# Key-value products of two token tiles in one run: eight runs instead of sixteen

## The chip, the cores and the metric

The kernel runs on one core of one Trainium2 chip. A core has a matrix engine (TensorE, PE in the profile; its weight loads are shown apart, as PEld), a vector engine (VectorE, DVE), a scalar engine (ScalarE, ACT), a general engine (GpSimd, POOL), and a queue engine that issues most transfers (SyncE, SP). Each works through its own list of instructions in order and waits on semaphores for the others. The metric is the device time of one execution, in microseconds; lower is better.

## The reference

The inputs are 2048 tokens of 640 numbers in float32. They are normalised over the 640; then two branches use the result, and the output combines them.

```python
xn = _layernorm(x, axis=-1)
s = _A_ref(xn, A_wqkv, A_w_phi, A_wo)          # attention branch
g = _silu(_B_ref(xn, B_w1, B_b1, B_w2, B_b2))  # 640 -> 1536 -> 640 with gelu
return x + s * g
```

The attention branch has 32 heads of 20 numbers and no softmax over tokens. Queries and keys go through a small weight per head and then through two softmaxes over the head's 20 numbers, one of the positive and one of the negative values, which gives 40 features per head. Keys and values meet in one sum over all tokens:

```python
phi_k = jnp.concatenate([_softmax(pk, axis=-1), _softmax(-pk, axis=-1)], axis=-1)
kv = jnp.einsum("bhsf,bhsd->bhfd", phi_k, v)
z  = jnp.einsum("bhsf->bhf", phi_k)
num = jnp.einsum("bhqf,bhfd->bhqd", phi_q, kv)
den = jnp.einsum("bhqf,bhf->bhq", phi_q, z)[..., None] + 1e-6
```

`kv` and `z` are 40 x 21 numbers per head, summed over 2048 tokens. This sum is what the change touches.

## The kernel before

The tokens are cut into 16 tiles of 128. The kernel has a first stage, in which keys, values and query features are made tile by tile, a feed-forward stage of 12 units (L870 on), and a last stage that forms the outputs. The first stage is the subject here.

For token tile t the first stage does the following. `project(t, wk_s)` (L323 to L336) makes the key projection with 30 matmuls of 320 columns, into a PSUM tile pA of two banks (`bankA`); there are three such tiles (`open_psum(early_psum, A=3, B=2)`, L79). `feat1` (L341) reads pA on VectorE (maximum L345, minimum L346, difference L349, L352) and makes the second half of the features on GpSimd (L353); L349 is the last to read pA. `value(t)` (L374) makes the value projection in another pA, which ScalarE copies to a row tile v (L380) with a column of ones per head, so that the same products give `z`. `feat2` takes the exponential on ScalarE (L358). `key_fin` (L389) sums per head on VectorE (L366), inverts (L391) and scales on GpSimd (L371); the result, phi, stays where e was. `query(t)` (L383) is a projection with `wq_s`, the same features, and a store to DRAM from ScalarE's queue (L385).

`kv_acc(t, phi, v)` (L395) then adds the tile to the sum. It issues 32 small matmuls: 128 tokens deep, 32 columns of weights from v, 40 moving columns from phi, each into one of four groups of 32 partitions of one PSUM bank (`kv`). They are in full float32, and each is shown in the profile as two matmuls and two weight loads, so that one call is 64 of each. The first call of all clears the sum (`start=t == 0`). Each of the 16 calls is one unbroken run at L403.

The order of the work is written out by hand, for all engines, in the order of the program text (`manual_schedule`, L462 and L468). Tiles 0 and 1 come first (L499 to L520), tiles 2 to 5 in one loop (L521), tiles 6 to 15 in another (L543). Before the change, the runs stand as follows: tile t - 2 after the key projection of tile t, for t = 2 to 5; tile 4 after the key projection of t = 6; and tile t - 1 at the end of each t from 6 on, behind a query projection (two query projections in t = 6, one in front and one behind in t = 7 to 9). Tile 15 is left for `kv_rest` (L597), after the loop, which also copies the sum out on ScalarE (L603). Around them stand the folds of the query weights (`fold_w`, L178: matmuls at L173, copies at L183 and L184), the statistics of later token tiles (`pair_stats`, L286: L197 to L202, L200 on GpSimd, a store to DRAM at L293 and a load of it back at L295, both on SyncE), the loads of token tiles (`x_in`, L455, issued at L141 on SyncE), and, for the second half of the tokens, the transposed x (xr, L231; subtracted at L301, multiplied at L306, split at L252 and L254) and its sums (tt, L267 and L284).

What sets the slots: the pool `slabs` (L50) has 23 slots, for the split weights, the features e and phi, xr, tt and the b12 pieces; the pool `rows` (L51) has 11, for token tiles, raw weights, v and the broadcast statistics. A slot is given out again when its last reader is done; the new writer waits for that reader.

The first feed-forward unit begins right behind the last query projection, with `part` (L640, matmuls at L650) on weights that `w1_forms` splits at the end of the loop (L415 to L427).

Of the kernel before, what the change touches and what calls it, by code (L numbers as in the profile page):

```python
# [16 lines left out]
NT = S // P  # L17
# [29 lines left out]
def hedgehog_gated_mlp_kernel(ctx: ExitStack, tc: tile.TileContext, x, xt_in, wqk, bd, wv, wo, w1, b1, w2, b2, out_t):  # L47
# [103 lines left out]
    def load_raw(src, blk=None):  # L151
        raw = row([P, D], F32, "raw")
        dst = raw[:] if blk is None else raw[:].rearrange("p (a b) -> p a b", b=blk)
        nc.sync.dma_start(dst, src)
        return raw
# [22 lines left out]
    def fold_w(tl, cs, name, dst):  # L178
        for c in cs:
            ps, mm = fold(tl, c)  # L180
            sl = slab(F32R, f"{name}{c}")
            s3 = sl[:].rearrange("p s (a b) -> p s a b", a=2)
            nc.scalar.activation(s3[:, 0], ps[:, :, :HALF], AF.Copy)  # L183
            lo = nc.vector.tensor_tensor(s3[:, 1], ps[:, :, :HALF], s3[:, 0].bitcast(F32), op=OP.subtract)  # L184
            dst.append(sl)
        return mm, lo
# [35 lines left out]
    def norm(t):  # L222
        norm_a(t)
        norm_b(t)
# [36 lines left out]
    def spill(q):  # L261
        nc.sync.dma_start(xp_dram[:, :8, :, at(q)], xp[:, :, :, at(q)].bitcast(F32))
        nc.sync.dma_start(xp_dram[:, 8:, :, at(q)], beside(q).bitcast(F32))
# [22 lines left out]
    def pair_stats(t):  # L286
        if t % 2 == 0:
            pst[0] = small.tile([P, 2, 2], F32, tag="pst", name="pst")
        sm = small.tile([P, 16], F32, tag="st", name="st")
        stats(t, sm, pst[0][:, t % 2, 0:1], pst[0][:, t % 2, 1:2])  # L290
        if t % 2:
            q = t // 2
            nc.sync.dma_start(st_dram[q].rearrange("i p s -> p i s"), pst[0][:])  # L293
            bc = row([P, W2, 2], F32, "bc")
            nc.sync.dma_start(bc[:].rearrange("p t s -> p (t s)"),  # L295
                              st_dram[q].rearrange("i p s -> (i p s)").partition_broadcast(P))
            pld[q] = bc
# [14 lines left out]
    def transpose_x(t):  # L312
        q, o = divmod(t, 2)
        xn = xns.pop(t)
        ps = bankA()
        flat = ps[:].rearrange("p a b -> p (a b)")
        for k in range(KC):
            nc.tensor.transpose(flat[:, k * P:(k + 1) * P], xn[:, k * P:(k + 1) * P], ident[:])  # L318
        plain(q, o, flat[:, :D].rearrange("p (k t) -> p k t", t=P))
# [3 lines left out]
    def project(t, ws, mid=None, at_k=3):  # L323
        q, o = divmod(t, 2)
        ps = bankA()
        n = 0
        for k in range(KC):
            if k == at_k and mid is not None:
                mid()
            for a, b in PASSES:  # L330
                for hf in range(2):
                    nc.tensor.matmul(ps[:, hf, :HALF], stat_x(q, o, k, a),  # L332
                                     ws[k][:, b, hf * HALF:(hf + 1) * HALF],
                                     start=n == 0, stop=n == 3 * KC - 1)
                n += 1
        return ps  # L336
# [4 lines left out]
    def feat1(ps):  # L341
        p4 = heads(ps)
        mx = small.tile([P, 2, 16], F32, tag="mx", name="mx")
        mn = small.tile([P, 2, 16], F32, tag="mn", name="mn")
        nc.vector.tensor_reduce(mx[:], p4, axis=AX.X, op=OP.max)  # L345
        nc.vector.tensor_reduce(mn[:], p4, axis=AX.X, op=OP.min)  # L346
        e = slab(F32, "e")[:]
        e5 = e.rearrange("p a (h s d) -> p a h s d", s=2, d=DH)
        nc.vector.tensor_tensor(e5[:, :, :, 0, :], p4, mx[:, :, :, None].to_broadcast([P, 2, 16, DH]),  # L349
                                op=OP.subtract)  # L350
        nr = small.tile([P, 2, 16], F32, tag="nr", name="nr")
        last_feat[0] = nc.vector.tensor_tensor(nr[:], mn[:], mx[:], op=OP.subtract)  # L352
        nc.gpsimd.tensor_tensor(e5[:, :, :, 1, :], nr[:, :, :, None].to_broadcast([P, 2, 16, DH]),  # L353
                                e5[:, :, :, 0, :], op=OP.subtract)
        return e.rearrange("p a b -> p (a b)")

    def feat2(ef):
        nc.scalar.activation(ef, ef, AF.Exp)  # L358
        return ef
# [14 lines left out]
    def value(t, mid=None):  # L374
        ps = project(t, wv_s, mid)
        v = row([P, VW], F32, "v")
        v3 = v[:, :32 * (DH + 1)].rearrange("p (h d) -> p h d", d=DH + 1)
        nc.gpsimd.memset(v3[:, :, DH:DH + 1], 1.0)
        nc.gpsimd.memset(v[:, 32 * (DH + 1):], 0.0)
        nc.scalar.activation(v3[:, :, :DH].rearrange("p (a h) d -> p a h d", a=2), heads(ps), AF.Copy)  # L380
        return v
# [13 lines left out]
    def kv_acc(t, phi, v):  # L395
        ps = kvp[0]
        for g in range(3):
            for r in range(3):
                for e in range(4):
                    h = 3 * (4 * g + e) + r  # L400
                    if 4 * g + e < NFT and h < H:
                        s = 3 * g + r
                        nc.tensor.matmul(ps[32 * e:32 * e + 32, 40 * s:40 * s + 40], v[:, 21 * h:21 * h + 32],  # L403
                                         phi[:, 40 * h:40 * h + 40], start=t == 0 and s == 0, stop=t == NT - 1,
                                         skip_group_check=True)

    vs, es, phis, xns, wk_s, wq_s = {}, {}, {}, {}, [], []

    def load_w1(g):
        return [load_raw(w1[f]) for f in range(g * GF, (g + 1) * GF)]  # L410

# [43 lines left out]
    def x_in(t):  # L455
        xts[t] = load_x(t)
# [63 lines left out]
    phis[1] = key_fin(es.pop(1))  # L520
    for t in range(2, 6):  # L521
        pk = project(t, wk_s)
        kv_acc(t - 2, phis.pop(t - 2), vs.pop(t - 2))
        es[t] = feat1(pk)
        if t == 5:
            fold_w(wqT, range(2, 3), "wq", wq_s)
        if t < 4:
            norm(t + 3)
        if t == 3:
            norm(7)  # L530
        if t > 3:
            pair_stats(t + 4)
        if t in (3, 4):
            spill(t - 3)
        if t == 5:
            x_in(10)
        vs[t] = value(t, (lambda: transpose_x(t + 2)) if t < 6 else None)
        feat2(es[t])
        if t >= 3:
            fold_w(wqT, range(t - 3 + (t > 4), t - 2 + (t > 4)), "wq", wq_s)  # L540
        phis[t] = key_fin(es.pop(t))
    queries = iter(range(NT))
    for t in range(6, NT):  # L543
        u = t + 4
        pk = project(t, wk_s)
        if t == 6:
            kv_acc(4, phis.pop(4), vs.pop(4))
        if u < NT:
            if u + 1 < NT:
                x_in(u + 1)  # L550
            pair_stats(u)
            if u % 2:
                load_xr(u // 2)
        if t in (6, 8):
            spill(t // 2 - 1)
        if t % 2 == 0 and 6 < t < NT - 2:
            pair_sub((t + 2) // 2)
        es[t] = feat1(pk)
        if t == 6:
            pair_sub(4)  # L560
            fold_w(wqT, range(4, KC), "wq", wq_s)
        if t % 2 == 0 and t < NT - 2:
            pair_mul((t + 2) // 2)
        if t == 12:
            w1r = load_w1(0)
        if t % 2 and t < NT - 2:
            t_sums((t + 1) // 2)
        vs[t] = value(t)
        feat2(es[t])
        phis[t] = key_fin(es.pop(t))  # L570
        if t % 2 == 0 and 6 < t < NT - 2:
            pair_plain((t + 2) // 2)
        if t % 2 and t < NT - 2:
            t_split((t + 1) // 2)
        if t == 6:
            query(next(queries))
            query(next(queries))
            pair_plain(4)
        if t == NT - 1:
            w1f = w1_forms(w1r)  # L580
            next(w1f)
            next(w1f)
        if t >= 7:
            query(next(queries))
        kv_acc(t - 1, phis.pop(t - 1), vs.pop(t - 1))
        if t == NT - 1:
            next(w1f)
        if 7 <= t < 10:
            query(next(queries))
    t = NT - 1  # L590
# [4 lines left out]
    w1g = next(w1f)  # L595

    def kv_rest():  # L597
        kv_acc(NT - 1, phis.pop(NT - 1), vs.pop(NT - 1))
        kvr = const.tile([P, 360], F32, name="kvr")
        nc.gpsimd.memset(kvr[64:96, 320:360], 0.0)  # L600
        nc.gpsimd.memset(kvr[96:, 240:360], 0.0)
        for p, a, b in ((P, 0, 240), (96, 240, 320), (64, 320, 360)):
            nc.scalar.activation(kvr[:p, a:b], kvp[0][:p, a:b], AF.Copy)  # L603
        return kvr
# [265 lines left out]
    for unit in range(units):  # L870
# [10 lines left out]
        if more and not back:  # L881
            w1r = load_w1((unit + 1) % NG)
# [206 lines left out]
```

## Time and profile before

| | |
|---|---|
| median of the runs | 684.15 us |
| lowest and highest of three runs | 682.97 and 684.3 us |
| profiled execution, first to last instruction (the span) | 681.1 us |
| the median less that span | 3.05 us |
| TensorE busy, share of the span | 676.4 us, 99% |
| VectorE, GpSimd, ScalarE busy | 454.8, 382.2, 253.0 us |
| granted TensorE clock | 1.000 |

The page gives the profiled execution by its span; what a run takes beside it is the third difference above. A row of the timeline is start, duration, engine, line, operation, the tile written and the tiles read, the shape and the count; in square brackets stands the idle time before it and what ended it. Matmuls overlap, so a TensorE that is shown as busy may still be slowed; the distance between the starts of two matmuls tells more than their durations. A row of the chain is start, duration, engine, tile, line and count.

### The profile page before, as it was taken

How to read it: one execution, taken by the hardware profiler on the slowest of the kernel's cores; microseconds unless marked ns; L12 is line 12 of the kernel's file. 1: busy time of each engine (PE TensorE's matmuls, PEld its weight loads, DVE VectorE, ACT ScalarE, POOL GpSimd, SP SyncE). 2: the span in 40 equal slices, each digit the busy share in tenths (PEclk: the TensorE clock that was granted, in tenths of full speed). 3: DMA queues.
4: the chain of work that ended last, by engine and by line, in shares of the span. 5: the costliest groups of instructions: out<-in, count | busy, mean ns of one | idle time of the engine just before them, and what ended most of it. 6: DMA issues, size and time to landing. Idle time of an engine off the chain costs nothing.

```text
span 681.1 us, 11991 instructions
## 1 busy us (share of the span) xinstructions
PE 676.4 (99%) x4727; PEld 592.0 (87%) x4727; DVE 454.8 (67%) x729; ACT 253.0 (37%) x400; POOL 382.2 (56%) x351
## 2 busy tenths in 40 slices
PE   9999999999999999999999999999999999999998
PEld 9999999999999998888888888888888887777876
DVE  5786665887876466586978784576876655774232
ACT  3523214333223337144254247533133254425440
POOL 3653254757767375857978952726446640783221
PEclk9999999999999999999999999999999999999999
DMA  8820144633451333329688696476363491888423
GB/s 330 311 80 1 11 142 100 227 93 137 69 200 60 115 138 135 117 88 348 209 273 278 237 426 280 129 259 224 139 216 137 151 398 47 321 296 291 150 94 109
DMA packets 73966, 125.42 MB, mean 184 GB/s; under 512 B 5822, under 2 KB 42686, under 8 KB 73014
## 3 DMA queue, kind: packets, MB, share of 16 engines
q1 hardware_dynamic: 71606, 114.17, 49.3%
q10 hardware_dynamic: 2304, 10.49, 4.4%
q8 instruction: 37, 0.61, 0.4%
q14 instruction: 19, 0.16, 0.1%
HBM read 79.54 MB, written 45.10 MB: 183 GB/s over the span
## 4 chain that ended last, share of the span: by engine, by line
PE 96%; DVE 1%; POOL 1%; issue 1%; ACT 0%; POOLq 0%
PE pA L332 30%; PE pB L679 24%; PE pB L650 22%; PE pB L844 11%; PE pB L780 3%; PE pB L769 2%; PE kv L403 2%; PE pA L173 1%; POOL wv L148 1%; PE pA L466 1%; PE pA L318 1%; PE pB L787 1%; DVE st L197 0%; DVE wk L184 0%; PE pB L624 0%
## 5 line engine op out<-in xcount | busy, mean ns | idle before, releaser
L679 PE MATMUL pB<-hs,w2s 128*128 128x512 f32 x720 | 167.1, 390 | 0.0
L679 PEld LDWEIGHTS pB<-hs,w2s 128*128 128x128 f32 x720 | 134.6, 188 | 29.4 <-PE pB L780 0.8
L650 PE MATMUL pB<-xp,w1s 128*128 128x512 f32 x324 | 81.4, 390 | 0.0
L650 PE MATMUL pB<-xd,w1s 128*128 128x512 f32 x324 | 79.3, 389 | 0.0
L358 ACT ACTIVATE e<-e 128x1280 f32<-128x1280 f32 x32 | 40.7, 1272 | 90.1 <-POOL e L353 89.5
L844 PE MATMUL pB<-oT,wo 128*128 128x512 f32 (+2 forms) x315 | 73.9, 386 | 0.0
L688 DVE TENSOR_TENSOR y<-pB,y 128x512 f32<-128x512 f32 x100 | 63.9, 680 | 12.4 <-PE pB L679 12.2
L650 PEld LDWEIGHTS pB<-xp,w1s 128*128 128x128 f32 x324 | 60.7, 188 | 12.9 <-DVE pB L925 0.4
L650 PEld LDWEIGHTS pB<-xd,w1s 128*128 128x128 f32 x324 | 60.8, 188 | 12.6
L844 PEld LDWEIGHTS pB<-oT,wo 128*128 128x128 f32 x315 | 57.1, 188 | 14.2 <-ACT ph L772 1.2
L371 POOL TENSOR_TENSOR e<-e,rc 128x1280 f32<-128x1280 f32 x16 | 39.0, 2438 | 48.8 <-DVE rc L391 48.4
L371 POOL TENSOR_TENSOR eq<-eq,rc 128x1280 f32<-128x1280 f32 x16 | 37.9, 2369 | 50.2 <-DVE rc L738 50.2
L353 POOL TENSOR_TENSOR e<-nr,e 128x640 f32<-128x640 f32 x32 | 45.5, 1424 | 30.1 <-DVE nr L352 27.7
L332 PE MATMUL pA<-wv,xp 128*128 128x320 f32 x384 | 60.7, 311 | 0.3 <-POOL wv L148 0.3
L655 ACT ACTIVATE pB<-pB,b1t 128x512 f32<-128x512 f32 x48 | 31.8, 662 | 77.2 <-DVE pB L925 27.6
L332 PE MATMUL pA<-wk,xp 128*128 128x320 f32 x384 | 59.9, 311 | 0.0
L332 PE MATMUL pA<-wq,xp 128*128 128x320 f32 x384 | 59.0, 309 | 0.0
L332 PEld LDWEIGHTS pA<-wv,xp 128*128 128x128 f32 x384 | 56.9, 188 | 0.6 <-POOL wv L148 0.5
L332 PEld LDWEIGHTS pA<-wq,xp 128*128 128x128 f32 x384 | 56.9, 188 | 0.1
L332 PEld LDWEIGHTS pA<-wk,xp 128*128 128x128 f32 x384 | 56.8, 188 | 0.1
L725 POOL TENSOR_TENSOR ez<-eq,zrep 128x1280 f32<-128x1280 f32 x16 | 47.3, 2959 | 0.2 <-PE pB L780 0.2
L427 POOL TENSOR_TENSOR w1s<-raw,w1s 128x640 fp32r<-128x640 f32 (+1 forms) x18 | 25.7, 1428 | 36.4 <-ACT w1s L426 29.2
(145 smaller groups left out, 1053.3 us busy)
## 6 DMA issues: line engine op xcount, KB each, us to landing
raw<-in_w_dram SPq DMA_DIRECT2D x42, 320.0 KB, 4.7
e_dram<-e ACTq DMA_DIRECT2D x16, 640.0 KB, 3.8
eq<-e_dram SPq DMA_DIRECT2D x16, 640.0 KB, 6.6
phi_dram<-eq SPq DMA_DIRECT2D x16, 640.0 KB, 3.5
phi<-phi_dram SPq DMA_DIRECT2D x16, 640.0 KB, 9.0
xt<-in_x_dram SPq DMA_DIRECT2D x16, 320.0 KB, 5.7
xres<-in_xt_dram SPq DMA_DIRECT2D x20, 256.0 KB, 4.3
out_dram<-xres SPq DMA_DIRECT2D x18, 256.0 KB, 3.0
```

Of the source, the lines that this page charges most:

```text
L332: nc.tensor.matmul(ps[:, hf, :HALF], stat_x(q, o, k, a), ws[k][:, b, hf * HALF:(hf + 1) * HALF], start=n == 0, stop=n == 3 * KC - 1)
L353: nc.gpsimd.tensor_tensor(e5[:, :, :, 1, :], nr[:, :, :, None].to_broadcast([P, 2, 16, DH]), e5[:, :, :, 0, :], op=OP.subtract)
L358: nc.scalar.activation(ef, ef, AF.Exp)
L371: nc.gpsimd.tensor_tensor(e3, e3, rc[:, :, None].to_broadcast([P, 64, DH]), op=OP.mult)
L427: nc.gpsimd.tensor_tensor(sl[:, 1, :n], src, sl[:, 0, :n].bitcast(F32), op=OP.subtract)
L650: nc.tensor.matmul(bank[ch][:], tl[:, a, off + wo_:off + wo_ + P], mov(blk, b), start=new and n == 0, stop=n == len(mms) - 1, skip_group_c ...
L655: nc.scalar.activation(ps, ps, AF.Gelu_apprx_tanh, bias=b1t[:, f:f + 1])
L679: nc.tensor.matmul(ps[:], ws[i][:, b, d * P:(d + 1) * P], hs[o][i][:, a, :], start=i == n == 0, stop=(i, n) == (GF - 1, 2), skip_group_che ...
L688: nc.vector.tensor_tensor(y, ps[:], y, op=OP.add)
L725: nc.gpsimd.tensor_tensor(zv, ef, zf, op=OP.mult)
L780: nc.tensor.matmul(po[64 * e:64 * e + 64, :256], bdk[:n, 2 * j + e, :], ph[:n, e * 256:(e + 1) * 256], start=True, stop=True)
L844: nc.tensor.matmul(ps[:, mv], w, o[:, mv], start=n == 0, stop=n == 15, skip_group_check=True)
```

## The change

The products of two token tiles are issued one after the other, in one run, where the odd tile's products were before. The even tile's are taken from their old place and put in front of the odd tile's. The second loop has no run in odd t; tiles 14 and 15 are both taken in `kv_rest`. No product is added or dropped, and the order of the sum is the same.

```diff
+    def kv_pair(t):
+        for u in (t, t + 1):
+            kv_acc(u, phis.pop(u), vs.pop(u))
...
     for t in range(2, 6):
         pk = project(t, wk_s)
-        kv_acc(t - 2, phis.pop(t - 2), vs.pop(t - 2))
+        if t % 2:
+            kv_pair(t - 3)
         es[t] = feat1(pk)
...
     for t in range(6, NT):
         u = t + 4
         pk = project(t, wk_s)
-        if t == 6:
-            kv_acc(4, phis.pop(4), vs.pop(4))
         if u < NT:
...
         if t >= 7:
             query(next(queries))
-        kv_acc(t - 1, phis.pop(t - 1), vs.pop(t - 1))
+        if t % 2 == 0:
+            kv_pair(t - 2)
         if t == NT - 1:
             next(w1f)
...
     def kv_rest():
-        kv_acc(NT - 1, phis.pop(NT - 1), vs.pop(NT - 1))
+        kv_pair(NT - 2)
```

## The prediction

> **What bounds the kernel now.** I read the page first, then the chain in order of time over the first stage, then the TensorE, VectorE and SyncE timelines around single key-value runs.
>
> ```profile
> span 681.1 us, 11991 instructions
> PE 676.4 (99%) x4727; PEld 592.0 (87%) x4727; DVE 454.8 (67%) x729; ACT 253.0 (37%) x400; POOL 382.2 (56%) x351
> PEclk9999999999999999999999999999999999999999
> PE 96%; DVE 1%; POOL 1%; issue 1%; ACT 0%; POOLq 0%
> ```
>
> TensorE is busy 99% of the span, holds 96% of the chain and runs at the full granted clock. So time taken off TensorE's row in the first stage (about 30 to 251 us) reaches the end, as long as no wait appears where there is none now. The chain shows what a key-value run costs; its columns are start, duration, line, count.
>
> ```profile
> 31.79 6.16 PE pA L332 x42
> 37.95 0.77 PE kv L403 x62
> 38.72 2.84 PE pA L332 x18
> ...
> 86.86 13.20 PE pA L332 x90
> 100.06 0.77 PE kv L403 x62
> 100.83 13.39 PE pA L332 x90
> ...
> 251.49 8.64 PE pB L650 x38
> ```
>
> The projections (L332) run at 6.16 / 42 = 0.1467 us each, and 13.20 / 90 gives the same. The 18 behind the run at 37.95 take 2.84 instead of 2.64, the 90 behind the one at 100.06 take 13.39 instead of 13.20. A run therefore costs its own 0.77 us and 0.2 us in the projections behind it: 0.97 us.
>
> **The change, part by part.** All 512 products stay, so does their order, and each still waits for a key tile that is ready early (the odd tile of a pair is used where it was used before). What goes is eight of the sixteen runs; what is added is a second half to each of the other eight.
>
> The price of a second half is not in the trace, as no run has two tiles. Its nearest rows are the inside of a run.
>
> ```profile
> 37.88 0.72 PEld L403 LDWEIGHTS kv<-e,v 128*32 128x32 f32 x64 [0.19 <-issue]
> 37.88 0.84 PE L403 MATMUL kv<-e,v 128*32 128x40 f32 x64
> L403 PEld LDWEIGHTS kv<-e,v x1024: 105/113/118, 37.9 to 246.7; 128*32 128x32 f32 x171
> L403 PE MATMUL kv<-e,v x1024: 202/202/224, 37.9 to 246.7; 128*32 128x40 f32 x171
> ```
>
> From the first to the last start there are 0.84 - 0.202 = 0.64 us on the matmul row and 0.72 - 0.113 = 0.61 us on the weight row, for 63 steps: 10.2 or 9.6 ns a step, 0.65 or 0.62 us for 64 more. I take 0.65, the row of the work itself. One merge then saves 0.97 - 0.65 = 0.32 us, eight save 2.56 us; with 0.62 it is 2.8. The ends are 0 (the second half costs a full 0.97) and 0.97 - 0.61 = 0.36, 2.9 in all. The 0.19 us in which the weight loader stands before the run, and the 0.2 behind it, are what a merge takes away.
>
> A rule of the Trainium skill speaks against the change: TensorEngine Tiling, section Instruction Overhead, gives every matmul about 60 cycles however small. At 2.4 GHz that is an estimate of 25 ns a step and 1.6 us for a second half, 0.63 us lost per merge, 689 us in all. The rows disagree: 10 ns a step, since the four column groups of 32 run beside each other (the same page's Key Properties say that tiles work independently); it stays as rival (e), with a price from the rows.
>
> Now the waits. Call the lead how much earlier TensorE reaches a place than before. Each removed run (tiles 0, 2, 4, ... 14) raises it by 0.97, each pair lowers it by 0.65: 0.97 behind tile 0's old place, 0.32 behind the first pair, 1.29, 0.64, and 1.61 behind the old place of tile 4 (t = 6). A wait shows where the lead of TensorE outgrows that of the work it waits for by more than the present cover. The one place is the first query projection, in t = 6.
>
> ```profile
> 84.49 0.84 PE L403 MATMUL kv<-e,v 128*32 128x40 f32 x64
> 85.26 1.60 PE L173 MATMUL pA<-folds 120*128 120x120 f32 x12
> 86.62 4.64 PE L332 MATMUL pA<-wv,xp 128*128 128x320 f32 x30
> 90.95 1.22 PEld L332 LDWEIGHTS pA<-wq,xp 128*128 128x128 f32 x8
> ...
> 73.92 0.71 ACT L183 ACTIVATE wq<-pA 128x640 fp32r<-128x640 f32 x1 [5.58 <-PE pA L173]
> 74.66 0.82 DVE L184 TENSOR_TENSOR wq<-pA,wq 128x640 fp32r<-128x640 f32 x1 [0.65 <-ACT wq L183]
> 76.62 0.15 DVE L202 COPY pst<-st 128x1 f32<-128x1 f32 x1
> 77.36 0.36 SPq L293 DMA_DIRECT2D st_dram<-pst  x1
> 81.22 0.86 SPq L141 DMA_DIRECT2D xt<-in_x_dram  x2
> 87.14 0.89 DVE L197 BATCH_NORM_STATS2 st<-xt 128x6 f32<-128x320 f32 x2 [2.93 <-DMA xt<-in_x_dram]
> 89.90 0.81 DVE L349 TENSOR_TENSOR e<-pA,mx 128x640 f32<-128x640 f32 x1
> ```
>
> There are three pA buffers; key projection 6, the weight fold, value projection 6 and this query take four in a row, so the query needs the buffer of key projection 6, which L349 on VectorE reads last, until 89.90 + 0.81 = 90.71. The query's first weight load is at 90.95: a cover of 0.24 us. VectorE is late for a reason that TensorE's earlier arrival does not mend: it stood 2.93 us at 87.14 for a token tile. That load was issued at 81.22, behind the statistics' store at 77.36, which waited for the copy at 76.62, behind L184 at 74.66, behind a fold that TensorE finished at 73.9, just after the pair of tiles 2 and 3. The lead there is 0.64, so the buffer comes free at 90.71 - 0.64 = 90.07. TensorE arrives with its lead of 1.61, at 89.34. It stops for 0.73 us (the removed run's 0.97 less the cover), plus the time to start again, for which no row stands; I take 0.8 together, with 0.5 and 1.1 as ends (the load's landing may shift by some tenths). The run of tile 4 now fills a gap there; once it is gone, the token tile's load is what is late.
>
> The next tight buffers I checked in the same way.
>
> ```profile
> 116.97 0.46 POOL L267 TENSOR_TENSOR tt<-xr 128x128 f32<-128x128 f32 x1
> 118.83 0.81 DVE L349 TENSOR_TENSOR e<-pA,mx 128x640 f32<-128x640 f32 x1
> 119.98 2.69 POOL L284 TENSOR_TENSOR xd<-tt,xd 128x1152 fp32r<-128x1152 f32 x1
> 139.72 0.81 DVE L349 TENSOR_TENSOR e<-pA,mx 128x640 f32<-128x640 f32 x1
> 142.39 1.92 PE L332 MATMUL pA<-wv,b 128*128 128x320 f32 x12
> 205.34 0.81 DVE L349 TENSOR_TENSOR e<-pA,mx 128x640 f32<-128x640 f32 x1
> 207.86 1.92 PE L332 MATMUL pA<-wq,b 128*128 128x320 f32 x12
> 250.96 1.29 POOL L427 TENSOR_TENSOR w1s<-st,w1s 128x512 fp32r<-128x512 f32 x1 [2.42 <-ACT w1s L426]
> 252.71 1.52 PE L650 MATMUL pB<-xd,w1s 128*128 128x512 f32 x6
> SPq L154 <- PE kv L403: 16.7, 2, 13.8
> ```
>
> At 142.39 the buffer is free at 140.53 (cover 1.86), at 207.86 at 206.15 (cover 1.71); behind the stop the leads there are 0.47 and 1.1, so the covers hold even if VectorE gained nothing. At the stage's end w1s is ready at 252.25 for a use at 252.71: cover 0.46, and the split follows value projection 15, whose lead is only 0.32 less than TensorE's. It holds, by 0.1.
>
> The kept tiles cost nothing by themselves while a slot is free. phi(6) holds its slab some 18 us longer, and around 114 us all 23 slabs are taken, by my count of the code's tiles: 15 split weights, three b12, two xr, phi(6), the features of key 7 and tt. Query 2's features (118.83) took phi(6)'s slab and now take another, the raw x tile's, free when L267 ends at 117.43. That covers it by 1.4 us; if they got tt's instead (L284 ends at 122.67), VectorE would stand 122.67 - 118.83 = 3.84 us. On SyncE two weight loads wait for rows that key-value runs free; tile 12's row comes free with the pair, one stretch of the chain later (13.39 + 0.77, 14 us: at about 227 instead of 213), for a load that the second feed-forward unit splits at 270.63. The next transfer behind it on SyncE starts at 234.71 for other reasons:
>
> ```profile
> 213.36 0.33 SPq L154 DMA_DIRECT2D raw<-in_w_dram  x1
> 234.71 0.61 SPq L699 DMA_DIRECT2D xhi<-xp_dram  x1
> ...
> 270.63 1.42 ACT L146 ACTIVATE w2s<-raw 128x640 fp32r<-128x640 f32 x2
> ```
>
> The sum: 2.56 - 0.8 = 1.76 us less of a span of 681.1, which lies 3.05 us under the median of the runs (684.15); I leave those 3.05 as they are: 682.4 us.
>
> **The rivals.** (a) No stop at the query: VectorE's load or copy gains as much as TensorE, or the cover is larger than it looks. For it: chains as long as this one seldom shift rigidly. Against it: the 2.93 us wait. Time 684.15 - 2.56 = 681.6. (b) The slab: query 2's features wait 3.84 us for tt. The delay runs through VectorE and GpSimd to 140.53, which becomes 140.53 - 0.64 + 3.84 = 143.7, against TensorE at 142.39 - 0.47 = 141.9: 1.8 us more of standing, 684.2, no change. Against it: the x tile's slab is free sooner. (c) Slower: each removed run was a filler, and a buffer wait takes its place everywhere as at the first query. Then the 0.97 is not gained in eight places and the 0.65 is added in eight: 8 x 0.65 = 5.2 us more, 689.3. The merges are eaten up from three full stops (2.9 us) on, and the kernel is over 0.2% slower from five. Against it: the covers of 1.7 to 1.9 us at the tightest other places. (d) The second half costs a whole run: no saving, 0.8 us of standing, 685.0. (e) The steps of a second half go one after another: the projections stream 320 columns in 0.1467 us, so 40 columns take 18 ns, 64 steps 1.17 us, 0.2 more than the run that went: 684.15 + 1.6 + 0.8 = 686.6. The Trainium skill's 60 cycles (above) are this rival with a higher price. Against both: a run's 64 steps now take 10 ns each.
>
> **How the numbers follow.** 0.2% (1.4 us) is about what a measurement of this kernel tells from no change, so faster means under 682.8 and slower over 685.5. Forecast, one stop: 50%, 681.9 to 683.0 with the bounds above (0.62 to 0.65 for a half, 0.5 to 1.1 for the stop); three quarters of it count as faster. (a) 20%, faster. (b) 13%, same. (c) 10%, slower, in part only: 686 to 689. (d) 5%, same. (e) 2%, slower. Faster 0.57, same 0.31, slower 0.12. The range reaches to (a) with its 2.9 us, 681.2, a little under for the runs' own spread, and up to (b) and (d): 681.0 to 685.0; it leaves out (c), (e) and some tails.
>
> **What would show it.** Eight L403 groups of 128, each 1.45 to 1.5 us long on the matmul row; a chain with one stop of TensorE ahead of the first query (about 89 to 91 us), named as VectorE's L349; and the feed-forward stage, L650, starting near 249.7 instead of 251.49. The forecast is wrong if the groups are longer than 1.55 us, if TensorE's row shows a wait at more places than one, or if VectorE's L349 of query 2 waits for GpSimd.

## The result, and the profile after

The changed kernel takes 680.6 us (median of five runs, 680.42 to 682.24) against 684.0 us for the kernel before on the same chip (682.97 to 684.3). The ratio over all these runs is 0.9961, with a 95% interval of 0.995 to 0.9973: 2.7 us faster of 684, 1.8 to 3.4 by the interval. The two medians alone lie 3.4 us apart, the upper end of that. The forecast was 682.4 us in a range of 681.0 to 685.0. Faster was right. The median lies 0.4 us under the range; the ratio, set against the 684.15 us from which the forecast was made, gives 681.5, inside it.

The page of the changed kernel, first its span and then what each engine was busy:

```profile
span 678.7 us, 11993 instructions
PE 673.7 (99%) x4727; PEld 591.3 (87%) x4727; DVE 456.4 (67%) x729; ACT 253.1 (37%) x400; POOL 382.1 (56%) x351
```

TensorE has the same 4727 matmuls and the same 99%. It is busy 2.7 us less, and the span is 2.4 us shorter. The chain of the kernel before has one row that is needed to line the two up (start, duration, engine, tile, line, count):

```profile
27.75 3.49 PE pA L332 x22
```

The chain of the changed kernel:

```profile
27.60 3.49 PE pA L332 x22
...
47.14 1.41 PE kv L403 x119
48.56 2.84 PE pA L332 x18
...
85.08 4.41 PE pA L332 x30
89.49 0.03 issue
89.52 9.03 PE pA L332 x60
98.55 1.42 PE kv L403 x116
...
249.03 11.13 PE pB L654 x49
```

The run of 22 projections at 27.60 stands 0.15 us earlier than before; no key-value run of either kernel lies ahead of it, so this is not the change. Counted from there, the feed-forward stage (L654, which was L650) starts after 221.43 us, where it started after 223.74 us: 2.31 us less. A run of two tiles is 1.41 us long in the chain where two single ones took 0.77 each, and the 18 projections behind it still take 2.84. A pair with its tail is 1.61 us, two singles with their tails 1.94: a merge saves 0.33 us. Eight save 2.6, and the missing 0.3 is at 89.49, where the chain leaves TensorE. The rows around that place, and three others that the prediction spoke of (VectorE's L349 of query 2, and the split and the use of w1s):

```profile
70.05 1.49 PE L403 MATMUL kv<-e,v 128*32 128x40 f32 x128
76.54 0.36 SPq L293 DMA_DIRECT2D st_dram<-pst  x1
79.44 0.33 SPq L295 DMA_DIRECT2D bc<-st_dram  x1
79.86 0.86 SPq L141 DMA_DIRECT2D xt<-in_x_dram  x2
84.81 4.40 PEld L332 LDWEIGHTS pA<-wv,xp 128*128 128x128 f32 x30
85.80 0.89 DVE L197 BATCH_NORM_STATS2 st<-xt 128x6 f32<-128x320 f32 x2 [2.40 <-DMA xt<-in_x_dram]
88.56 0.81 DVE L349 TENSOR_TENSOR e<-pA,mx 128x640 f32<-128x640 f32 x1
89.49 4.40 PEld L332 LDWEIGHTS pA<-wq,xp 128*128 128x128 f32 x30 [0.28 <-PE pA L332]
117.60 0.81 DVE L349 TENSOR_TENSOR e<-pA,mx 128x640 f32<-128x640 f32 x1
248.82 1.30 POOL L431 TENSOR_TENSOR w1s<-st,w1s 128x512 fp32r<-128x512 f32 x1 [2.42 <-ACT w1s L430]
250.25 1.52 PE L654 MATMUL pB<-xd,w1s 128*128 128x512 f32 x6
```

The query's weight loads stand 0.28 us, from 89.21 to 89.49, and start 0.12 us behind the end of L349 of key 6 (89.37). The row names the projection before it (PE pA L332) as what ended the wait, not L349 as the prediction expected; that L349 sets it is shown below by the early load. VectorE still stood 2.40 us for the token tile at 85.80. Query 2's L349 has no wait at all, and w1s is ready at 250.12 for a use at 250.25. Two rows of the waits show what else moved, TensorE's first and SyncE's second (total, times, longest):

```profile
PE pB L784 <- DVE oT L788: 0.3, 1, 0.3
SPq L154 <- PE kv L403: 29.7, 3, 27.0
```

TensorE has a wait of 0.3 us in the last stage that the profiled execution of before did not have. The early load below does not have it, and a kernel with sixteen runs (the control below) has it, so it does not belong to the change.

### The profile page after: what moved, and what is told of

It is laid out like the page before. It is cut to its first block, busy times and chain, and to the rows that moved or that the text cites. A ratio compares the mean times of both kernels' runs of the same rounds, so it can differ in the third digit from the quotient of the medians.

```text
span 678.7 us, 11993 instructions
## 1 busy us (share of the span) xinstructions
PE 673.7 (99%) x4727; PEld 591.3 (87%) x4727; DVE 456.4 (67%) x729; ACT 253.1 (37%) x400; POOL 382.1 (56%) x351
## 4 chain that ended last, share of the span: by engine, by line
PE 93%; DMA 3%; DVE 2%; POOL 1%; issue 1%; SPq 0%; ACT 0%; DVEq 0%; POOLq 0%
PE pA L332 30%; PE pB L683 23%; PE pB L654 20%; PE pB L848 11%; PE pB L784 3%; PE kv L403 2%; PE pB L773 2%; DMA raw<-in_wo_dram 2%; DMA phi<-phi_dram 1%; PE pA L173 1%; POOL wv L148 1%; PE pA L470 1%; PE pA L318 1%; PE pB L791 1%; DVE st L197 0%
## 5 line engine op out<-in xcount | busy, mean ns | idle before, releaser
L654 PE MATMUL pB<-xp,w1s 128*128 128x512 f32 x324 | 81.3, 389 | 0.0
L654 PE MATMUL pB<-xd,w1s 128*128 128x512 f32 x324 | 79.3, 389 | 0.0
L654 PEld LDWEIGHTS pB<-xd,w1s 128*128 128x128 f32 x324 | 60.8, 188 | 12.6
L654 PEld LDWEIGHTS pB<-xp,w1s 128*128 128x128 f32 x324 | 60.7, 188 | 12.7 <-DVE pB L929 0.2
L332 PE MATMUL pA<-wv,xp 128*128 128x320 f32 x384 | 60.5, 310 | 0.3 <-POOL wv L148 0.3
L332 PE MATMUL pA<-wk,xp 128*128 128x320 f32 x384 | 59.6, 310 | 0.0
L332 PE MATMUL pA<-wq,xp 128*128 128x320 f32 x384 | 58.8, 309 | 0.0
L332 PEld LDWEIGHTS pA<-wv,xp 128*128 128x128 f32 x384 | 57.0, 188 | 0.5 <-POOL wv L148 0.5
L332 PEld LDWEIGHTS pA<-wq,xp 128*128 128x128 f32 x384 | 56.9, 188 | 0.3 <-PE pA L332 0.3
L332 PEld LDWEIGHTS pA<-wk,xp 128*128 128x128 f32 x384 | 56.9, 188 | 0.0
```

Source lines behind the costliest of these rows:

```text
L332: nc.tensor.matmul(ps[:, hf, :HALF], stat_x(q, o, k, a), ws[k][:, b, hf * HALF:(hf + 1) * HALF], start=n == 0, stop=n == 3 * KC - 1)
L654: nc.tensor.matmul(bank[ch][:], tl[:, a, off + wo_:off + wo_ + P], mov(blk, b), start=new and n == 0, stop=n == len(mms) - 1, skip_group_c ...
```

## The experiments

All readings below are set against one place each, the start of the 22 projections near 28 us, because the whole trace lies up to 0.9 us earlier or later from run to run, ahead of the first key-value run. The table gives for each kernel that start, the start of the feed-forward stage, and how the difference of the two stands to that of the kernel before. It can tell tenths of a microsecond; the medians of whole runs can't tell less than about 1 us. Ratios are to the kernel before on the same chip; where a kernel ran once, its time stands in their place, beside medians of 683.1 to 683.3 us for the kernel before.

| kernel | runs of key-value products | 22 projections at | feed-forward at | against before | ratio (95% interval) |
|---|---|---|---|---|---|
| before | 16 | 27.75 | 251.49 | | |
| changed | 8 | 27.60 | 249.03 | -2.31 | 0.9961 (0.995 to 0.9973) |
| early_load | 8 | 27.96 | 249.11 | -2.59 | 0.9954 (0.994 to 0.9967) |
| before_early | 16 | 27.34 | 251.14 | +0.06 | 0.9995 (0.9987 to 1.0004) |
| single45 | 9 | 27.59 | 249.08 | -2.25 | 680.55 us, once |
| split31 | 31 | 27.75 | 256.14 | +4.65 | 1.0067 (1.0052 to 1.0083) |
| serial | 8 | 27.78 | 269.36 | +17.84 | 700.54 us, once |
| pair_ahead | 8 | 28.23 | 250.11 | -1.86 | 0.9966 (0.9954 to 0.9979) |
| ahead_shift | 8 | 28.18 | 249.60 | -2.32 | 681.03 us, once |
| ahead_spill | 8 | 27.68 | 249.83 | -1.59 | 681.32 us, once |
| five_runs | 5 | 28.06 | 257.52 | +5.72 | 1.0112 (1.0095 to 1.0129) |
| five_serial | 5 | 27.50 | 269.63 | +18.39 | 703.16 us, once |
| seven_a | 7 | 28.20 | 249.02 | -2.92 | 0.9959 (0.9946 to 0.9971) |
| seven_b | 7 | 27.61 | 253.62 | +2.27 | 1.005 (1.0037 to 1.0062) |

### The stop at the first query: early_load, before_early, single45

early_load, in the loop over t = 2 to 5:

```diff
+        if t == 5:
+            x_in(10)
         if t > 3:
             pair_stats(t + 4)
...
-        if t == 5:
-            x_in(10)
         vs[t] = value(t, ...)
```

> The changed kernel, with one transfer moved: the load of token tile 10 is issued on SyncE ahead of the statistics' store and load of tiles 8 and 9, not behind them. Theory (the 0.28 us in which TensorE stands ahead of the first query projection comes from VectorE, which stands 2.40 us for this token tile): VectorE no longer stands there, L349 of key 6 is done before 88.5 instead of 89.37, the 0.28 us are gone, and the feed-forward stage starts 0.28 us earlier than in the changed kernel, 2.6 us earlier than before, which is 8 x 0.325. Rival (the stop has another cause, in the fold or in the projections' own order): 0.2 to 0.3 us of standing stay, and the stage starts 2.3 us earlier than before.

VectorE no longer waits, and the chain passes the place unbroken. VectorE's row and the chain's:

```profile
86.37 0.82 DVE L349 TENSOR_TENSOR e<-pA,mx 128x640 f32<-128x640 f32 x1
```

```profile
85.43 13.20 PE pA L332 x90
```

The stage starts 2.59 us earlier than before, 8 x 0.324: the stop is the token tile's load, and with it gone the eight merges are the whole gain.

before_early has the same edit on the kernel before.

> The kernel before, sixteen runs, with the same early load of token tile 10. Theory: VectorE's wait of 2.93 us goes, but TensorE did not stand there, as tile 4's run filled the wait (cover 0.24 us): ratio 1.000, the feed-forward stage starts where it did, within 0.1 us. Rival (the transfers' times by themselves made part of the gain): 0.2 us or more faster.

The stage moves by 0.06 us and the ratio is 0.9995. The load alone is worth nothing, since tile 4's run covered the wait.

single45 puts tile 4's run back behind the key projection of t = 6, and tile 5's behind the queries:

```diff
         pk = project(t, wk_s)
+        if t == 6:
+            kv_acc(4, phis.pop(4), vs.pop(4))
...
-        if t % 2 == 0:
+        if t == 6:
+            kv_acc(5, phis.pop(5), vs.pop(5))
+        elif t % 2 == 0:
             kv_pair(t - 2)
```

> The changed kernel, with tiles 4 and 5 back in two runs at their old places: seven pairs and two single runs. Theory: tile 4's run fills the wait of 0.28 us again, and one merge of 0.33 us is lost, so the feed-forward stage starts 0.05 us later than in the changed kernel: 2.26 us earlier than before. Rival (tile 4's run filled nothing): the stop of 0.28 us stays and the merge is lost, 2.0 us earlier than before. Rival (a single run among pairs costs nothing more): 2.6 us earlier than before.

2.25 us earlier than before, where 2.26 was expected. Tile 4's run and the stop exchange 0.33 for 0.28 us.

### What a run costs, and why a step takes 10 ns: split31, serial

split31 cuts each tile's products in two, but for the last tile's, from the kernel before:

```diff
     def kv_acc(t, phi, v, part):
...
                         s = 3 * g + r
+                        if (s >= 4) != (part == 1):
+                            continue
```

> The kernel before, with the products of each tile but the last cut into two runs of 16 products, one of them at the old place and the other one projection away from it: 31 runs. No product goes or is added. Theory (a run entered and left costs 0.32 to 0.33 us whatever its length, and a step 10 ns): 15 runs more, 4.8 to 5.0 us, so the feed-forward stage starts 4.9 us later than before and the ratio is 1.007; a run of 16 products is 0.52 us long on the matmul row in place of 0.84. Rival (the cost is in the products alone): no change. Rival (part of the cost is the wait for the first product's data, which a second half would not pay): less than 3 us.

The chain around the two halves of one tile:

```profile
101.99 0.48 PE kv L405 x32
102.47 8.99 PE pA L332 x60
111.46 0.42 PE kv L405 x32
111.89 4.59 PE pA L332 x30
```

The 60 projections take 8.99 us in place of 8.80, the 30 take 4.59 in place of 4.40. The two halves with their tails are 0.48 + 0.19 + 0.42 + 0.19 = 1.28 us, a whole run is 0.97: 0.31 us for one more run. Fifteen more cost 4.65 us, a little less than the 4.9 expected. The cost of a run that is entered and left is thus nearly the same from 7 to 31 runs. What it is made of is not shown, beyond the rows: the weight loader stands 0.19 us ahead of a run, of one tile or of two, and the projections behind it take 0.2 us more.

serial changes the order of the products in a run, not their number:

```diff
-        for g in range(3):
-            for r in range(3):
-                for e in range(4):
+        for e in range(4):
+            for g in range(3):
+                for r in range(3):
```

> The changed kernel with the products of a tile in another order: all that go to the first group of 32 partitions, then the second, third and fourth, where before each product went to another group than the one ahead of it. Theory (a step takes 10 ns because products in different groups run beside each other): in one group they go one after another, at least the 18 ns that 40 columns take at the projections' rate; a run of 128 takes 2.5 us or more in place of 1.49, 8 us or more in all. A rule that would give more: the Trainium skill (TensorEngine Tiling, Instruction Overhead) has some 60 cycles for a matmul, by which an estimate is 25 ns a step and 15 us in all. Rival (10 ns is the rate at which TensorE issues, whatever the group): groups of 1.5 us and no change.

```profile
47.32 3.90 PE kv L403 x128
```

A run of 128 takes 3.90 us in the chain, 30 ns a step, and the stage starts 20.15 us later than in the changed kernel: 8 x (3.90 - 1.42) = 19.8, and a stop at the first query of 0.59 us in place of 0.28. The 10 ns of a step come from products that go to different groups of 32 partitions. For products that stay in one group the 18 ns of the projections' rate were too low. So were the 25 ns estimated from the rule of the Trainium skill (TensorEngine Tiling (Array Packing), section Instruction Overhead).

### A stop that nothing explains at first: pair_ahead, ahead_shift, ahead_spill

pair_ahead was meant as another filler for the wait at the first query:

```diff
         if t == 6:
+            kv_pair(4)
             query(next(queries))
...
-        if t % 2 == 0:
+        if t % 2 == 0 and t > 6:
             kv_pair(t - 2)
```

> The changed kernel, with the run of tiles 4 and 5 moved from behind the two query projections of t = 6 to a place ahead of them. Theory (any work of TensorE that stands there fills the buffer wait, and what a run costs does not depend on its place): no stop, eight merges of 0.32 to 0.33 us kept, the feed-forward stage starts 2.6 us earlier than before. Rival (the merges were worth less than 0.33 us, and some of the gain came from the place that tile 4's run left): the stage starts less than 2.3 us earlier than before. Rival (phi of tile 5 is late for this place): a stop of TensorE at L403.

The wait for pA is filled, but the run itself is broken, and the page names no releaser:

```profile
90.11 1.41 PE kv L403 x117
91.52 0.47 issue
91.99 0.26 PE kv L403 x2
```

Only 1.86 us are left of 2.6. The two last matmuls of the run have no wait in the trace. What stands near is a packet of 16 KB on queue q8, whose kind the page calls "instruction", from 89.57 to 90.45. The next run moves TensorE's code by 16 instructions: it makes the warm-up loop at L469 seven long in place of five.

> The kernel with the pair of tiles 4 and 5 ahead of the queries, and four more warm-up matmuls at the very start, in which each call is two matmuls and two weight loads, 16 instructions in all. The stop of 0.47 us there came with 126 of the run's 128 matmuls done. Theory (TensorE waits for its code, which comes in blocks of instructions): the stop moves 16 instructions forward in the program, to 118 matmuls done, and grows by the time in which those 16 were issued, 0.09 us, to about 0.55 us. Rival (it waits for data or for a buffer): the stop stays behind 126 matmuls.

```profile
90.06 1.29 PE kv L403 x109
91.34 0.06 issue
91.40 0.34 PE kv L403 x10
```

The break moved from 117 to 109 of the chain's matmuls, eight matmuls and eight weight loads, as the code theory says and no wait for data would. Its size was expected wrongly: 0.06 us and a slower tail (0.27 us of the stage in all), not 0.55. The packet also began earlier, at 89.21, 0.85 us ahead of the run in place of 0.54.

ahead_spill moves `spill(2)` behind the queries of t = 6.

> The kernel with the pair of tiles 4 and 5 ahead of the queries, and the store of the split x of token pair 2 (1.25 MB, issued on SyncE in t = 6) moved behind the two queries. Theory (the code block is late because the transfer engines are 90% busy and more with that store and a token tile from 86 to 91 us): the block comes earlier, the stop of 0.47 us shrinks to under 0.2 us or goes, and the feed-forward stage starts 2.6 us earlier than before. Rival (the block is late for its size or for the time of its request, whatever else the transfer engines do): 0.4 us or more stay.

```profile
90.96 0.75 issue
```

The stop grew. This run doesn't settle whether busy transfers delay a block: between 87 and 89.4 us the transfer engines moved 349 GB/s in it and 348 GB/s without the edit, so the edit took no load away where it mattered. The packet began at 89.48, only 0.07 us ahead of the run, where it was 0.54 us in pair_ahead, and TensorE went on 2.2 us behind its start (2.4 in pair_ahead). So the stop grew with the lateness of the packet; what made the packet late is not shown.

### Longer runs: five_runs, five_serial, seven_a, seven_b

five_runs takes the early load, and a list of the tiles of each run by its place:

```diff
+    RUNS = {5: (0, 1, 2, 3), 6: (4, 5), 10: (6, 7, 8, 9), 14: (10, 11, 12, 13), 16: (14, 15)}
+
+    def kv_run(t):
+        for u in RUNS.get(t, ()):
+            kv_acc(u, phis.pop(u), vs.pop(u))
```

> The changed kernel with the early load of token tile 10, and five runs in place of eight: tiles 0 to 3, 4 and 5, 6 to 9, 10 to 13, 14 and 15. Theory (each run that goes saves 0.32 to 0.33 us, as long as no wait comes): three more go, 1.0 us, and the feed-forward stage starts 3.55 us earlier than before (2.59 with eight runs), ratio to before 0.994. Rival (slabs): phi of tiles 6 and 7 hold two more slabs through the stretch in which all 23 are taken, so features or tt wait, VectorE is late by some us, and TensorE stands at a projection for pA. Rival (code): the kernel with the pair ahead of the queries showed TensorE standing 0.47 us two matmuls before its run's end, with nothing that it waits for; its instructions come in blocks of 16 KB, 256 instructions, on queue q8, and a run of four tiles uses two blocks in 2.8 us. If a block takes longer to come than 1.4 us, TensorE stands inside the runs of four tiles, by 0.5 us or more each, and nothing is gained or time is lost.

It is 1.1% slower. Its chain (the first stop falls just behind the first run of four, in the matmuls of a fold):

```profile
72.19 1.27 issue
...
167.66 2.63 PE kv L403 x224
170.29 2.14 issue
172.43 0.27 PE kv L403 x5
172.70 54.55 PE pA L332 x360
```

Counting TensorE's matmuls and weight loads in the trace, its four stops come after 1473, 3521, 4545 and 4801 of them, and those of pair_ahead and ahead_spill after 1985 (the expectations count one less): all differ by multiples of 256. Each ends 2.2 to 2.7 us after a packet of q8 begins (71.15 for the restart at 73.47, 169.80 for 172.43), while a run uses up 256 instructions in 1.42 us. The four stops are 4.2 us of the 9.3 by which the kernel missed its forecast. A further part is a slower clock: the 360 projections from 172.70 on take 54.55 us, not 52.8 + 0.2. The view by stretches has the granted clock as the third number from the end:

```profile
174.00:176.00 2.00, 2.00 (x9) 2.00 (x9) 1.97 (x4) 0.30 (x1) 0.80 (x1) 0.50 0.00 0
```

The third part is one wait of another kind, at the start of the feed-forward stage:

```profile
PE pB L654 <- DVE nr L352: 2.5, 1, 2.5
```

L352 comes right behind L349, the last reader of the last query's pA, so a PSUM bank that the stage's first tile takes over from that pA would explain it; no row shows the banks. In the changed kernel the stage begins (249.03) before that L349 is done (251.35) and doesn't wait. The slabs cost nothing: no projection waits for a slab or for VectorE to free pA. Stops, clock and this wait are 8.2 of the 9.3 us; the rest stays unexplained.

five_serial is five_runs with the order of serial.

> Five runs, with the products ordered by partition group, so that a step takes 30 ns (a run of 128 took 3.90 us in the changed kernel with that order) and a block of 256 instructions lasts 3.9 us in place of 1.4. Theory (the stops in the runs of four tiles come from using code faster than it is delivered): no stop of 0.25 us or more inside the runs, each run of four tiles about 7.8 us. Rival (the runs of four wait for phi or v of their last tiles): stops of the same places and sizes stay.

```profile
172.78 7.56 PE kv L403 x256
```

All three runs of four tiles are 7.56 us and unbroken. The same runs, of the same length and data, do not stand when a block lasts 3.9 us.

seven_a and seven_b have the early load and two runs of three tiles, which begin at different distances from the borders of 256. seven_a:

```diff
+    RUNS = {3: (0, 1), 5: (2, 3), 6: (4, 5), 8: (6, 7), 10: (8, 9), 13: (10, 11, 12), 16: (13, 14, 15)}
```

seven_b:

```diff
+    RUNS = {3: (0, 1), 5: (2, 3), 6: (4, 5), 8: (6, 7), 11: (8, 9, 10), 14: (11, 12, 13), 16: (14, 15)}
```

> The changed kernel with the early load, and seven runs: 0 and 1, 2 and 3, 4 and 5, 6 and 7, 8 and 9, 10 to 12 (t = 13), 13 to 15. The stops in the kernel with five runs came after 1472, 3520, 4544 and 4800 of TensorE's matmuls and weight loads, and with the pair ahead of the queries after 1984: all steps of 256 apart, and the first block of queue q8 that holds the code was there 2.3 to 2.7 us after its packet began. Theory (a run stands when it uses up a whole block, 1.4 us, before the next is there): by the count the run of 10 to 12 begins after 4076 and meets one border, 4288; that of 13 to 15 begins after 4885 and meets one, 5056. Neither holds a whole block, so none stands: one switch less than with eight runs, the feed-forward stage starts 2.9 us earlier than before, ratio 0.995. Rival (any run longer than a pair stands for its length): one stop of 0.3 us or more in each of the two, nothing gained over eight runs. Rival (slabs): VectorE late, TensorE stands for pA.

```profile
209.31 2.06 PE kv L403 x176
...
242.37 2.06 PE kv L403 x174
```

No stop, and 2.92 us earlier than before, 9 x 0.324. The median, 680.28 us against 683.11 for the kernel before beside it (ratio 0.9959), can't be told from that of the changed kernel.

> The same with the long runs elsewhere: 0 and 1, 2 and 3, 4 and 5, 6 and 7, 8 to 10 (t = 11), 11 to 13 (t = 14), 14 and 15. Theory (code blocks): the run of 8 to 10 begins after 3456 matmuls and weight loads and meets two borders, 3520 and 3776, so it holds a whole block: it stands after 3776, for 0.5 to 1.0 us. The run of 11 to 13 begins after 4386, meets only 4544, and does not stand. The feed-forward stage starts 1.9 to 2.4 us earlier than before. Rival (length alone): both stand alike. Rival (no wait for code): neither stands, and the stage starts 2.9 us earlier.

```profile
180.71 1.70 PE kv L403 x144
182.41 0.22 issue
182.64 0.20 PE kv L403
182.84 3.06 issue
...
186.64 41.12 PE pA L332 x270
227.76 2.06 PE kv L403 x176
```

The run of 8 to 10 stands at the border expected (3776), and that of 11 to 13 does not. The size was far off: 3.06 us, not 0.5 to 1.0. The block's packet came late; the transfers between 183.4 and 184.5 us have its row, those between 181 and 183.4 have none:

```profile
q8 instruction: 1, 0.02, 5.0%
```

It began at 183.52 and the run went on at 185.90, 2.4 us later, as elsewhere. Why it began 1.1 us after TensorE had first stood stays open. From 181 to 183.4 us the packets of queue q1 took 99.9% of the transfer engines' time, so a delay by other transfers is possible, but not shown. The clock fell here too, so that the 270 projections took 1.3 us more than 39.8. The 0.53 is a mean that takes in the first 0.1 us at full clock; from 186.2 to 189.4 us it was 0.50:

```profile
186.00:188.00 2.00, 2.00 (x37) 1.91 (x38) 1.59 (x2) 0.34 (x1) 1.92 (x4) 0.53 1.05 369
```

## Why the prediction was right in kind and short in size

**The saving of a merge** (0.97 less 0.65) was right: 0.33 in the chain, and 0.324 each where nothing else stands (early_load). A second half takes 1.49 - 0.84 = 0.65 us on the matmul row, the value taken from the spacing of steps. Rivals (d) and (e) fall with it. serial shows what (e) would have needed: products of one group behind each other.

**The stop** was at the place, for the reason and the only one in the first stage: ahead of the first query projection, behind L349 of key 6, held up by the token tile. single45 and early_load show both sides of it. Its size was the first term that failed: 0.28 us in place of 0.8, of which 0.16 are the wait for L349 and 0.12 the time to start again. TensorE's arrival was right: 89.34 forecast, 89.21 measured, which is 89.36 with the 0.15 us by which this trace starts earlier. The buffer came free at 89.37, or 89.52 so counted, not at 90.07. The 0.55 us between are nearly all in the statistics' way out to DRAM, which the prediction took as rigid. The row of before

```profile
80.79 0.33 SPq L295 DMA_DIRECT2D bc<-st_dram  x1
```

follows its store (77.36) by 3.43 us; in the changed kernel it is 79.44 after 76.54, 2.90 us. Rival (a) had the reason right, that chains as long as this one seldom shift rigidly, but not its outcome, no stop at all. Why the store landed 0.53 us sooner is not shown.

**The base** was the second term that failed, and the larger one. The prediction laid 3.05 us between span and run and left them as they are. That was the median of three runs less the span of one of them, two different executions. The profiled run of the changed kernel took 680.42 us for a span of 678.7: 1.72 us. The same 1.7 lie beside the spans of the other kernels (682.7 for 681.0 in before_early), so by this the profiled execution of before took about 682.8, a little under the fastest of its three runs (682.97). With that base the forecast would have been 682.8 - 1.76 = 681.1. The other 0.5 us is the stop. The high median of before is not one stray run: five runs gave 684.0 on that chip, while on the other chips 7 to 17 runs gave 683.1 to 683.3. Why before was 0.7 to 0.9 us slower there is not known. The traces give the change 2.3 us in the first stage and 2.4 us in the span; no row accounts for the rest of the 3.4 us between the medians.

**What was called free** was free: the covers of 1.86 and 1.71 us and that of 0.46 at the end of the stage held, the last with 0.13 us left (0.1 forecast). Query 2's features did not wait, so rival (b) falls. Tile 12's row was freed 13 us later (27.0 us on SyncE in place of 13.8) and nothing waited for its load. Rival (c) falls with the covers. What the prediction had not seen at all is the code: a run of two tiles is 256 instructions, a whole block. None of the eight stands, though the same pair at another place (pair_ahead) did: the block behind a run has to be there in time, and what sets when its packet begins stays open. So it was luck, as far as the prediction goes, that the change lost nothing here.

## What to carry to other kernels

Join short runs of small products: each run entered and left cost 0.31 to 0.33 us here beside its steps, whatever its length. Do it only up to the length at which the engine's own code keeps up, and before a run is removed, look whether it fills a wait, and mend the load behind the wait first. Set a forecast from a trace against the time of the traced execution; a median of other executions adds their scatter, here 1.3 us.

## What the runs showed of the hardware

TensorE's code comes in blocks of 256 instructions, and at the eight stops the next block could be used 2.2 to 2.7 us after its packet on q8 began. At 5.5 ns an instruction (256 in 1.42 us) the key-value runs use it up faster; at 15 ns (serial) they don't. The Trainium skill's Runtime: NRT & Kernel Launch, section Instruction fetch mechanics, has blocks of 16 KiB or 256 instructions, with which the borders agree, and calls the crossing mostly hidden, since issue is slower than the refill. The measurements differ on that: here it cost up to 3.06 us at a time.

A stop of 2.14 us (five_runs) and one of 3.06 us (seven_b) each brought the granted clock of TensorE to 0.50 for about 3.4 us, beginning 1.4 and 0.2 us behind the stop, and cost 1.3 to 1.5 us more; after stops of up to 1.3 us it stayed at 1.00. The length of the stop alone doesn't decide it. Ahead of the feed-forward stage five_runs and five_serial have the same idle stretch on the matmul row, 2.47 us: behind it the clock stayed at 1.00 in five_runs (257.6 to 261 us), and was 0.50 in five_serial (270.4 to 273.6 us). The Trainium skill's TensorE: Matmul & The Clock Gate, section Why this matters for your kernels, warns of idle gaps over about 3 us; 2.14 us were enough once and 2.47 us were not another time, so the measurement goes ahead of that figure.
